# One chunk of attention moved to 64-row matmuls with three swaps of row tiles, and the u loads moved to another queue

## Chip, cores, metric

One core of a Trainium2 chip. The metric is the device time of one execution in microseconds (us). The profile's engines are PE (TensorE), DVE (VectorE), ACT (ScalarE), POOL (GpSimd) and SP (SyncE). A "q" behind an engine is its sequencer; the number behind L is a line of that run's kernel, so the same statement has other numbers before and after.

## The reference, cut to what matters

```python
# batch 8, seq S = 3008, d_model 256, d_qk 64; d_ff 2048
scores = (1.0 / S) * (z @ z.T)            # per batch
attn   = np.maximum(scores, 0.0) ** 2
x      = u * (attn @ v)                   # gated attention, (8*3008, 256)
h      = x @ w_in
out    = (h * sigmoid(1.702 * h)) @ w_out
```

The queries go in chunks of 512 (six a batch), the keys in 24 blocks of 128; the last key block holds 64 rows. A "score unit" is a pair of key blocks against one chunk. Scores are symmetric, so a chunk takes the blocks left of its diagonal from transposed squares of earlier chunks (tiles `tt`, made by DMA transposes that SyncE issues).

## The kernel before

`post` and `behind` are the only ordering between the two array halves: `post` is a GpSimd instruction that waits for the last matmuls of one half assignment, and `behind` makes the first matmuls of the next wait for it.

```python
TOP, LOW, FULL = slice(0, SREM), slice(SREM, P), slice(0, P)      # 0:64, 64:128, 0:128

def post(last):
    sig = pool.nop()
    for m in last:
        tc.add_manual_dep(sig.ins, m.ins.name, SYNC, reason="row tiles of one bank")
    return sig

def load_u(b, i):
    eng = pool if b or i else sp
    # ... four DMAs into uq (two buffers)

def scores(b, group):        # 64-row matmuls: two per unit, side by side in the array
    # ... pe.matmul(sc[:, r, :], zt[r * 64:(r + 1) * 64, key block], zt[same rows, chunk])

def square(b, i, jp, sc):    # ScalarE: relu(sc) -> rl; VectorE: rl * rl -> a; then, for some, a transpose of a into tt

def attend(b, i, both=False):
    # ... js: the key blocks in this chunk's order; cs: the two halves of the 256 channels
    half = [(0, TOP, NJ - 1), (1, LOW, NJ - 1)]
    if both:                 # chunks 0 and 1 of batch 0
        order = [[(c, FULL, j)] for j in js[:-CB] for c in cs] + [[(c, FULL, j)] for c in cs for j in js[-CB:]]
        order.insert(-CB, half)
    elif i == full(b):
        ...
    else:                    # all blocks in one half assignment, swap, all blocks in the other
        order = [[(0, TOP, j), (1, LOW, j)] for j in js] + [half] + [[(1, TOP, j), (0, LOW, j)] for j in js]
    acc, turn = {}, -1 if both or i == full(b) else NJ
    def step(k):
        for m in order[k]:
            # ... ins = pe.matmul(acc[c], V16[h, j] (channels c), weights(b, i, j)[h])
            if k == turn:
                behind(acc["sig"], ins)
        if k == turn - 1:
            acc["sig"] = post(done)

SCHED0 = {                   # chunk: {step: score units issued ahead of it}
    1: {0: 2, 8: 2, 15: 2, 22: 2, 30: 2, 38: 2},
    # ...
}
LOAD0 = {(1, 14): 2, (2, 12): 3, (2, NJ + 20): 4, (4, 8): 5}      # (chunk, step): u tile to load
LOADW = {(2, 16): 0, (2, 30): 1, (3, 9): 2, (3, 41): 3, ...}      # quarters of w_in, from GpSimd

# in the main loop, for every batch:
if i == 3 and n in (3, 26) and LAST2:
    LAST2.pop(0)()           # two late stores of the batch before, from SyncE's queue
```

## Time and profile before

| | before |
|---|---|
| time, median of 3 at first | 1180.64 us (1180.62 to 1186.32) |
| PE busy | 99% of the span |
| chunk 1, first score to the next chunk's first score | 37.64 - 23.36 = 14.28 us |
| transposes of `tt` in the first 80 us, issue to landing | 5.2 us median, 8.9 at most |

TensorE is the bound. The prediction shows its lines.

### The profile page before, as it was taken

How to read it: one execution, taken by the hardware profiler on the slowest of the kernel's cores; microseconds unless marked ns; L12 is line 12 of the kernel's file. 1: busy time of each engine (PE TensorE's matmuls, PEld its weight loads, DVE VectorE, ACT ScalarE, POOL GpSimd, SP SyncE). 2: the span in 40 equal slices, each digit the busy share in tenths (PEclk: the TensorE clock that was granted, in tenths of full speed). 3: DMA queues.
4: the chain of work that ended last, by engine and by line, in shares of the span. 5: the costliest groups of instructions: out<-in, count | busy, mean ns of one | idle time of the engine just before them, and what ended most of it. 6: DMA issues, size and time to landing. Idle time of an engine off the chain costs nothing.

```text
span 1178.7 us, 23495 instructions
## 1 busy us (share of the span) xinstructions
PE 1172.5 (99%) x9238; PEld 667.2 (57%) x9238; DVE 870.7 (74%) x1455; ACT 849.6 (72%) x1033; POOL 222.1 (19%) x313
## 2 busy tenths in 40 slices
PE   9999999999999999999999999999999999999998
PEld 3446664466644675446654467544674446744566
DVE  6779866878758786587875878658786587764776
ACT  7888874688746887478864787647876478772785
POOL 5243101231012310132101431014100241001000
PEclk9999999999999999999999999999999999999999
DMA  9998679877698677976879668896578965796023
GB/s 226 217 120 125 133 116 160 91 112 135 106 156 100 108 135 130 150 91 95 147 128 149 94 93 157 139 137 94 94 135 135 141 106 97 127 158 127 1 37 73
DMA packets 449696, 143.66 MB, mean 122 GB/s; under 512 B 414640, under 2 KB 443056, under 8 KB 449584
## 3 DMA queue, kind: packets, MB, share of 16 engines
q1 hardware_dynamic: 392160, 99.80, 51.2%
q0 software_dynamic: 56064, 41.04, 23.1%
q8 instruction: 72, 1.18, 0.4%
q10 hardware_dynamic: 1360, 1.31, 0.4%
q14 instruction: 40, 0.33, 0.1%
HBM read 60.29 MB, written 24.64 MB: 72 GB/s over the span
## 4 chain that ended last, share of the span: by engine, by line
PE 99%; ACT 1%; issue 0%; DVE 0%
PE o L358 40%; PE hg L399 27%; PE st L523 23%; PE sc L235 6%; PE st L526 1%; PE yp L497 1%; PE w L99 0%; ACT rl L256 0%; ACT W L443 0%; ACT gf L407 0%; PE zp L135 0%; ACT ZT L143 0%; ACT zst L126 0%; DVE y L544 0%; DVE nil L75 0%
## 5 line engine op out<-in xcount | busy, mean ns | idle before, releaser
L407 ACT ACTIVATE gf<-hg 128x1024 f32<-128x1024 f32 (+1 forms) x384 | 385.5, 1004 | 113.6 <-PE hg L399 98.3
L256 ACT ACTIVATE rl<-sc 128x1024 f16<-128x1024 f32 (+1 forms) x301 | 287.5, 993 | 145.4 <-PE sc L235 101.2
L358 PEld LDWEIGHTS <-V 64*128 64x128 f16 (+1 forms) x4052 | 217.7, 94 | 253.9 <-issue 11.8
L399 PE MATMUL hg<-xt,W 128*128 128x512 f16 (+1 forms) x1408 | 354.6, 374 | 0.2
L358 PE MATMUL o<-a,V 64*128 64x512 f16 (+3 forms) x2240 | 296.0, 368 | 0.0
L411 DVE TENSOR_SCALAR gt<-gf 128x1024 f16<-128x1024 f32 (+1 forms) x288 | 203.0, 705 | 114.0 <-ACT gf L407 112.8
L195 POOL DMA_DIRECT2D uq<-in_u_dram x188 | 125.2, 674 | 751.8 <-PE sc L235 527.5
L270 DVE TENSOR_TENSOR a<-rl 128x1024 f16<-128x1024 f16 (+1 forms) x266 | 177.6, 670 | 112.3 <-ACT rl L256 111.0
L358 PE MATMUL o<-tt,V 64*128 64x512 f16 (+1 forms) x1510 | 232.2, 377 | 0.0
L399 PEld LDWEIGHTS <-W 128*128 128x128 f16 x1536 | 149.4, 98 | 125.6 <-issue 2.6
L523 PEld LDWEIGHTS <-WT 128*128 128x128 f16 x1472 | 139.1, 98 | 45.1
L523 PEld LDWEIGHTS <-W 128*128 128x128 f16 x1104 | 104.7, 98 | 32.2
L235 PE MATMUL sc<-ZT 64*128 64x512 f16 (+3 forms) x688 | 115.5, 357 | 0.5 <-ACT ZT L143 0.3
L409 ACT ACTIVATE gt<-gf 128x1024 f16<-128x1024 f32 (+1 forms) x96 | 98.9, 1030 | 3.0
L540 ACT ACTIVATE y<-st 128x256 f32<-128x256 f32 x192 | 70.8, 369 | 35.7 <-PE st L523 29.2
L523 PE MATMUL st<-gt,WT 128*128 128x256 f16 (+1 forms) x736 | 91.9, 268 | 0.0
L523 PE MATMUL st<-s,WT 128*128 128x256 f16 (+1 forms) x736 | 90.8, 268 | 0.0
L523 PE MATMUL st<-gt,W 128*128 128x256 f16 (+1 forms) x736 | 90.8, 268 | 0.0
L544 DVE SCALAR_TENSOR_TENSOR y<-st,y 128x256 f32<-128x256 f32 (+1 forms) x144 | 57.7, 407 | 24.3 <-ACT y L540 11.7
L375 DVE TENSOR_TENSOR xt<-o,ut 128x512 f16<-128x512 f32 x80 | 51.3, 683 | 28.5 <-PE o L358 28.5
L477 DVE TENSOR_TENSOR s<-s,gt 128x1024 f16<-128x1024 f16 (+1 forms) x96 | 63.7, 663 | 1.1
L475 DVE TENSOR_TENSOR s<-gt 128x1024 f16<-128x1024 f16 (+1 forms) x96 | 63.3, 660 | 0.0
(59 smaller groups left out, 668.5 us busy)
## 6 DMA issues: line engine op xcount, KB each, us to landing
uq<-in_u_dram POOLq DMA_DIRECT2D x156, 128.0 KB, 3.6
out_dram<-yo SPq DMA_DIRECT2D x156, 128.0 KB, 2.8
V<-in_v_dram POOLq DMA_DIRECT2D x35, 256.0 KB, 6.4
tt<-a SPq DMA_TRANSPOSE x232, 3.4
uq<-in_u_dram POOLq DMA_DIRECT2D x32, 112.0 KB, 5.4
out_dram<-yo SPq DMA_DIRECT2D x28, 96.0 KB, 6.0
wst<-in_moe_w_in_dram POOLq DMA_DIRECT2D x4, 512.0 KB, 6.2
vst<-in_v_dram SPq DMA_DIRECT2D x3, 512.0 KB, 5.4
```

Of the source, the lines that this page charges most:

```text
L195: eng.dma_start(uq[k * QW:(k + 1) * QW, :n // QW].rearrange("t q c k -> t q (c k)"), src[:, :, cs])
L235: pe.matmul(sc[:, r, :q1 - q0], zt[h, 2 * kp + r, :], zt[h].rearrange("d n p -> d (n p)")[:, q0:q1], start=True, stop=True,)
L256: act.activation(rl[:, :, :n], sc[:, :, :n], AF.Relu, scale=csc)
L270: dve.tensor_tensor(a[:, :, :n], rl[:, :, :n], rl[:, :, :n], ALU.mult)
L358: ins = pe.matmul(acc[c][:, :n], V16[b][h, j].rearrange("p (c k) -> p k c", k=NCC)[:, c], weights(b, i, j)[h], start=(k, m) == first[c], s ...
L399: pe.matmul(hg[:, e, :n], W1[:, c, ff * P:(ff + 1) * P], XT[b, i][:, c, :n], start=(c == 0), stop=(c == NCC - 1),)
L407: act.activation(gf[:, :, :n], hg[:, :, :n], AF.Gelu_apprx_sigmoid, scale=1.0 / FSC)
L409: act.activation(g, gf[:, :, :n], AF.Copy, scale=FSC)
L411: dve.tensor_scalar(g, gf[:, :, :n], FSC, None, ALU.mult)
L477: dve.tensor_tensor(s_, ST[b, k, "S1", h], a11, ALU.subtract)
L523: pe.matmul(bank, right[:, ff], lhs()[:, f], start=first, stop=last, skip_group_check=True)
L540: act.activation(y[:, c, :, o], bank, AF.Copy, scale=1.0 / FSC)
```

## The change

A 64-row matmul uses half of the rows of TensorE's array, a "row tile", so that two of them run side by side; a "swap" exchanges which half of the array adds to which output bank.

Intent: of the three 128-row chunks of the first batch, chunk 1 goes to 64-row matmuls, so that TensorE need not change mode around each score group. Its score units come while the chunk runs, so not all key blocks are there in the first half of it; therefore the blocks go in groups, with three swaps at steps 8, 22 and 38, each behind two score units. The first batch's u tiles come from SyncE's queue, which frees GpSimd for the swap signals, and the second weight quarter is held until chunk 2 is done.

```diff
     def load_u(b, i):
-        eng = pool if b or i else sp
+        eng = pool if b else sp
@@ attend
-        if both:
+        turns = [NJ]
+        if (b, i) == (0, 1):
+            x, y = ([(0, TOP), (1, LOW)], [(1, TOP), (0, LOW)])
+            parts = [(x, js[:8]), (y, js[:14]), (x, js[8:]), (y, js[14:])]
+            order = [[(c, h, j) for c, h in cfg] for cfg, part in parts for j in part]
+            order.insert(37, half)
+            turns = [8, 22, 38]
+        elif both:
@@ step
-                if k == turn:
+                if k in turns:
                     behind(acc["sig"], ins)
-            if k == turn - 1:
+            if k + 1 in turns:
                 acc["sig"] = post(done)
@@ load_w
-        if k == 0:
-            hold = const.tile([P, 1], F16, name="hold")
-            pool.tensor_copy(hold, XT[0, 1][:, 0, :1])
+        if k < 2:
+            hold = const.tile([P, 1], F16, name=f"hold{k}")
+            pool.tensor_copy(hold, XT[0, k + 1][:, 0, :1])
@@ LOADW
-        (2, 16): 0, (2, 30): 1, (3, 9): 2, ...
+        (2, 16): 0, (3, 0): 1, (3, 9): 2, ...
@@ ahead of the main loop
-    load_u(0, 1)
@@ main loop
-            for n, step in enumerate(attend(b, i, b == 0 and i < 2)):
-                if b == 0 and i == 0 and n == 5:
-                    load_u(0, 0)
+            for n, step in enumerate(attend(b, i, b == 0 and i == 0)):
+                if b == 0 and i == 0 and n in (5, 24):
+                    load_u(0, n // 24)
```

More of the change, by code (lines that the diff above doesn't have):

```diff
@@ L349, in attend @@
         final = {c: [m for m in flat if m[1][0] == c][-1] for c in cs}
-        acc, turn = {}, -1 if both or i == full(b) else NJ
+        acc = {}
+        if both or i == full(b):
+            turns = []
         def step(k):
@@ L623 @@
     LOADW = {
-        (2, 16): 0, (2, 30): 1, (3, 9): 2, (3, 41): 3, (4, 28): 4, (4, 34): 5, (4, 40): 6, (5, 0): 7,
+        (2, 16): 0, (3, 0): 1, (3, 9): 2, (3, 41): 3, (4, 28): 4, (4, 34): 5, (4, 40): 6, (5, 0): 7,
     }
```

## The prediction

> **What bounds the kernel now.** I read the page's busy shares and the chain that ended last first, then the matmul engine's timeline over the first two chunks of the first batch, then ScalarE's and GpSimd's over the same stretch.
>
> ```profile
> PE 1172.5 (99%) x9238; PEld 667.2 (57%) x9238; DVE 870.7 (74%) x1455; ACT 849.6 (72%) x1033; POOL 222.1 (19%) x313
> ...
> PE 99%; ACT 1%; issue 0%; DVE 0%
> ```
>
> TensorE is 99% of the span and 99% of the chain, at a granted clock of 1.00. So only what shortens PE's own stream counts, and a microsecond taken out of it shows at the end unless a later wait eats it. The "busy" hides something, though: modelled matmul ends overlap the next start, so a pause of 0.1 us between two matmuls counts as busy. Start times show it. Here is chunk 1 of batch 0 (start, length, instruction group):
>
> ```profile
> 23.36 0.61 PE L235 MATMUL sc<-ZT 64*128 64x512 f16 x4
> 23.89 1.90 PE L358 MATMUL o<-tt,V 128*128 128x512 f16 x8
> 25.73 0.61 PE L235 MATMUL sc<-ZT 64*128 64x512 f16 x4
> 26.27 1.69 PE L358 MATMUL o<-a,V 128*128 128x512 f16 x7
> 27.88 0.66 PE L235 MATMUL sc<-ZT 64*128 64x512 f16 x4
> 28.47 1.69 PE L358 MATMUL o<-a,V 128*128 128x512 f16 x7
> 30.09 0.61 PE L235 MATMUL sc<-ZT 64*128 64x512 f16 x4
> 30.63 1.90 PE L358 MATMUL o<-a,V 128*128 128x512 f16 x8
> 32.46 0.61 PE L235 MATMUL sc<-ZT 64*128 64x512 f16 x4
> 33.00 1.90 PE L358 MATMUL o<-a,V 128*128 128x512 f16 x8
> 34.84 0.60 PE L235 MATMUL sc<-ZT 64*128 64x512 f16 x4
> 35.37 2.33 PE L358 MATMUL o<-a,V 128*128 128x512 f16 x10
> 37.64 0.39 PE L235 MATMUL sc<-ZT 64*128 64x512 f16 x2
> ```
>
> The next chunk already runs in 64-row mode:
>
> ```profile
> 41.10 2.75 PE L358 MATMUL o<-a,V 64*128 64x512 f16 x24
> 43.69 0.59 PE L235 MATMUL sc<-ZT 64*128 64x512 f16 x4
> 44.12 1.03 PE L358 MATMUL o<-a,V 64*128 64x512 f16 x8
> 44.99 0.38 PE L358 MATMUL o<-tt,V 64*128 64x512 f16 x2
> ```
>
> Two 64-row matmuls start together, so I count "passes" of 512 columns: one full matmul, or one pair of 64-row ones. The x24 group is 12 passes in 43.69-41.10 = 2.59 us, 0.2158 us a pass. A full matmul costs the same within a mode. But in chunk 1 the cycle from score group to score group is 25.73-23.36 = 2.37 us for 8 full passes and 2 score passes, which at 0.2158 would be 2.16: 0.21 us more. The x7 cycle 25.73 to 27.88 is 2.15 against 9 x 0.2158 = 1.94, again 0.21. The loss is per trip out of full mode and back, not per pass. In chunk 2 there is none: 44.12 to 44.99 is 4 passes in 0.87 us, and the score group before it took 0.43 for 2.
>
> **What the Trainium skill says.** "TensorEngine Tiling (Array Packing)", Key Properties: changing the tiling mode, not just the tile, drains TensorE. The trace agrees: 0.21 us per round trip. The same page, Gotcha 1: different row tiles cannot access one PSUM bank at once and software must synchronize; that is why the 64-row order keeps each half of the array on its own output bank and needs a signal when the halves are exchanged. "TensorE: Matmul & The Clock Gate", Part 3, The mechanism: tiles of different row groups overlap, starting about 4 ns apart; the trace agrees, with a pair taking one pass of 0.2158 us. "DMA: Bandwidth & Descriptors", Issuing engines are not separate DMA queues: moving an issue only saves the issuing sequencer's time, the 16 engines stay shared. For the u move I rely on that; here one u issue takes 0.65 us of GpSimd and 0.48 to 0.57 us of SyncE.
>
> **The change part by part.**
>
> *Chunk 1's attention in 64-row mode.* The work is unchanged: 46 block-passes plus the half block is 47, plus 12 score units of one pass each, 59 passes, 59 x 0.2158 = 12.73 us. The chunk takes 37.64-23.36 = 14.28 us. The excess is 1.55 us: six trips to the score groups and one to the half block inside the x10 group (its cycle, 34.84 to 37.64, is 2.80 against 11 x 0.2158 = 2.37, so 0.43, two trips), 7 x 0.21 = 1.49, and a wait of 0.05 in the group at 27.88 (0.66 where the others take 0.61). The change removes all seven; the one switch on leaving chunk 0 lies before 23.36 and stays, with some 0.01 us of it in the first score pass. TensorE gets 94 attention matmuls for 48, so the matmul count goes 9238 to 9284, at no cost in time.
>
> *Three swaps.* At steps 8, 22 and 38 (and score units also at 0, 15 and 30) the halves are exchanged. Each swap waits for the last pair, by way of a GpSimd signal. Chunk 2's swap, shown above, is the same thing under the same cover of two score units: last pass, 0.43 us of scores, next pass at 44.12 with no hole. I put the three swaps at 0, if GpSimd is free (below).
>
> *What the faster stream runs into: ScalarE.* It must empty two score banks per group:
>
> ```profile
> 26.16 1.94 ACT L256 ACTIVATE rl<-sc 128x1024 f16<-128x1024 f32 x2 [0.43 <-PE sc L235]
> 28.32 1.94 ACT L256 ACTIVATE rl<-sc 128x1024 f16<-128x1024 f32 x2 [0.22 <-PE sc L235]
> ```
>
> ScalarE starts 0.43 after a score group does and is done 1.94 later; about 0.05 after that the group's second bank can be written. So the second unit of the next group may start no sooner than 2.42 us after the first unit of this one (25.73+2.42 = 28.15, which is where the 0.05 wait comes from: it wanted to start at 28.11). After the change, groups 8 steps apart are 10 passes = 2.16 us, the second unit wants to start at 2.37: waits 0.04 to 0.05. Groups 7 steps apart, 8 to 15 and 15 to 22, are 9 passes = 1.94, second unit at 2.16 to 2.19: a wait of about 0.23 to 0.26 for the first. It pushes the group itself back, so the interval to 22 is already ScalarE's own pace (1.94) and costs about nothing more. From 22 to 30 0.05 again, then nothing. Sum: 0.035 + 0.23 + 0.045 = 0.31 us. ScalarE's total of 12 x 0.97 = 11.6 us for the chunk stays under 12.7, so it doesn't become the bound of the chunk, only of this spot.
>
> New length: 12.73 + 0.01 + 0.31 = 13.05 us. Gain 14.28 - 13.05 = 1.23 us.
>
> *GpSimd, the u and weight loads.*
>
> ```profile
> 17.21 2.71 POOL L195 DMA_DIRECT2D uq<-in_u_dram  x4
> 22.72 2.58 POOL L195 DMA_DIRECT2D uq<-in_u_dram  x4 [2.80 <-DVE ut L202]
> 34.63 2.58 POOL L195 DMA_DIRECT2D uq<-in_u_dram  x4 [9.33 <-DVE ut L202]
> ```
>
> GpSimd runs in order, so a signal stuck behind an issue that waits would stop TensorE. After the change: signal 1 at about 25.3, then the loads of u chunk 2 (their buffer was released at 22.7 already), 4 x 0.65 = 2.6 us to about 28.1; signal 2 is due at about 29.5, signal 3 at about 33. Both find GpSimd idle. Chunk 1's own u, from SyncE, is issued after the transposes that end at 19.2 and lands well before it is turned (33.1 before, some 0.8 us sooner now). The second weight quarter moves from 44.6 to the end of chunk 2, about 49.8; a quarter takes 5.5 to 7.3 us to land, so by 57, and its cast stands at 61.56 now, 60.3 then. None of this is on the path: 0.
>
> *Beyond.* Everything after 37.64 starts 1.23 us sooner. PE has no wait for a DMA anywhere later in this trace, and batches 1 to 7 are untouched. I keep the whole 1.23: 1180.64 - 1.23 = 1179.4.
>
> **Rivals.**
> 1. *The swap signal becomes the new wait.* For: each goes TensorE, GpSimd, TensorE, and GpSimd issues loads between signals 1 and 2. Against: 1.4 us of slack there, and chunk 2's swap shows no hole. If each of the three cost 0.4 us, the gain would be eaten: 1180.6.
> 2. *ScalarE or VectorE paces chunk 1 more than I think.* VectorE is busy 10.5 of the 14.28 us, including a transposition of 1.24 us, and a late square holds a ScalarE output buffer. That would cost another 0.2 to 0.5: 1179.7 to 1179.9.
> 3. *Transfers give it back.* The DMA engines are near full up to 70 us, that load doesn't shrink, and demands come 1.23 us sooner. Transposed tiles take 3.4 us from issue to landing over the kernel, up to 8.9 here. Those of chunk 1's first blocks, issued from 25.6 on, are needed by chunk 2 at about 38.8; those of chunk 2's, issued at 37 to 40, by chunk 3 near 52.6. There are some microseconds of slack at each, and the weight casts follow ScalarE's order, not their landing. If it did bite, 1179.8 to 1180.6. A better result (1179.1) would need ScalarE's wait to be absent.
>
> **Range and chances.** The mechanism is measured in this trace and its ceiling is the 1.55 us of excess (1179.1); only the ScalarE wait and the swaps are uncertain. The three times before are 1180.62, 1180.64 and 1186.32, so repeats usually agree to 0.02 but one can lie far off. 1178.9 to 1180.7 should hold the median 8 times in 10. A gain of 0.1% cannot reach 2% (23.6 us) either way: within 2% 0.99, slower 0.005, faster 0.005.
>
> **What would show it.** In the changed profile: in chunk 1 only 64x512 attention groups, score groups of 4 lasting 0.59 instead of 0.61, and the chunk from first score to next chunk's first score 13.05 us; a longer score group (about 0.8) at step 15; no hole after the score groups at steps 8, 22 and 38; PE x9284; u issues on GpSimd 184 instead of 188. I am wrong on the swaps if attention starts over 0.5 us after its score group there; wrong on ScalarE if step 15's group shows no wait or several groups do; wrong on the rest if chunk 1 shrinks by 1.2 us and the span doesn't, with a new wait for tt, W or ut in chunks 2 to 4.

## The result and the profile after

Six runs: 1180.38 us median (1179.89 to 1181.13), beside 1180.55 before (1180.33 to 1186.32 over six). The ratio of the fast runs is 0.9992, 95% interval 0.9975 to 1.0009: the same. (That of the medians quoted here would be 0.9999.) The time lies in the predicted range, but of the 1.23 us that the prediction wanted to keep, the medians show 0.17. Times alone settle nothing at this size: the interval is some 2 us wide to each side, and what follows is read from one profiled run of each kernel.

Chunk 1 did what was predicted. The timeline of TensorE after (start, length, group):

```profile
23.24 0.61 PE L235 MATMUL sc<-ZT 64*128 64x512 f16 x4
23.68 1.03 PE L367 MATMUL o<-tt,V 64*128 64x512 f16 x8
...
27.38 0.83 PE L235 MATMUL sc<-ZT 64*128 64x512 f16 x4
28.03 1.69 PE L367 MATMUL o<-a,V 64*128 64x512 f16 x14
29.54 0.66 PE L235 MATMUL sc<-ZT 64*128 64x512 f16 x4
30.02 1.90 PE L367 MATMUL o<-a,V 64*128 64x512 f16 x16
...
36.32 0.40 PE L235 MATMUL sc<-ZT 64*128 64x512 f16 x2
```

36.32 - 23.24 = 13.08 us, for 14.28 before: 1.20 us less. The group at 27.38 is step 15's, with ScalarE's wait in it (0.83 for 0.61). Behind the swap group at 29.54 attention goes on after 0.48 us, with no hole.

Matched matmul by matmul, the changed kernel is 1.32 us ahead at 36.32 (0.12 of it from before chunk 1, within what that start varies from run to run), and it is still 1.33 ahead at the last batch's chunk 4, where its score pair starts at 1075.26 and that of before at 1076.59. One score pair later it is ahead by only 0.21 (1081.31 and 1081.52). The timeline of before there:

```profile
1080.23 0.60 PE L358 MATMUL o<-ad,V 64*128 64x512 f16 x4
1080.66 1.03 PE L358 MATMUL o<-tt,V 64*128 64x512 f16 x8
```

and of after:

```profile
1078.90 0.59 PE L367 MATMUL o<-ad,V 64*128 64x512 f16 x4
1080.44 1.04 PE L367 MATMUL o<-tt,V 64*128 64x512 f16 x8 [0.94 <-DMA tt<-a]
```

Four 64-row matmuls are two passes, 0.43 us; 1078.90 + 0.43 = 1079.33, so TensorE stood for 1.11 us, waiting for a transposed tile. The chain of waits after shows the way to it (start, length, what):

```profile
1073.18 0.63 DVE a L270
...
1075.24 0.47 SPq L599
...
1075.83 4.57 DMA tt<-a
```

The square was ready at 1073.95 (after a small second VectorE step), four stores stood ahead in SyncE's queue until 1075.7, and the transpose took 4.57 us. In the kernel before it was issued 1.44 us later (1077.27) and took 3.14, so it landed at the same 1080.4. Why did it take longer? The DMA view of the stretch 1077 to 1079.5 us after has one 16 KB transfer of the instruction queue that the view of 1077.3 to 1080.4 before doesn't have. Its row of digits is the busy share of the DMA engines in 40 slices, the row below what they moved:

```profile
DMA  7799999999999999991990000001000100100000
GB/s 140 152 188 193 221 213 209 229 471 233 205 213 225 197 209 164 119 66 25 29 8 0 0 0 0 0 0 8 4 8 8 12 8 8 12 8 8 8 12 12
...
q8 instruction: 1, 0.02, 2.9%
```

The fetch begins at 1077.56 and takes 1.17 us; some twenty of the transpose's 256-byte packets, which take 20 ns elsewhere, end only after 1.3 to 1.6 us; then the engines move almost nothing until 1079.5. While before's transpose was under way, no 256-byte packet took over 0.1 us. The whole trace of after says the same: of the 385,408 such packets in the same hardware queue 488 took over 1 us, and 466 of these began during one of the 72 fetches, which cover 79 us of the 1178. (Not every fetch does it: 25 of the 72 held up ten packets or more.) That suggested theory A: the gain was real, and a fetch of TensorE's instructions, shifted by the change onto the last tight transpose, gave it back.

"Runtime: NRT & Kernel Launch", Instruction fetch mechanics, in the Trainium skill says that instructions are refilled in 16 KiB blocks of 256, each sequencer driving its own DMA queue. The trace agrees: 72 such transfers for TensorE's 2 x 9284 weight loads and matmuls, one per 258. The change adds 46 matmuls and 46 weight loads, 92 instructions, so each later fetch comes 92 instructions earlier in the program. In 64-row mode four instructions take 0.2158 us, so 92 take some 5.0; with the 1.3 us lead, the fetch at 1083.6 before should come near 1077.3. It came at 1077.6.

### The profile page after: what moved, and what is told of

Its sections match the earlier page's. It is cut to its first block, busy times and chain, and to the rows that moved or that the text cites. A ratio compares the mean times of both kernels' runs of the same rounds, so it can differ in the third digit from the quotient of the medians.

```text
span 1178.3 us, 23585 instructions
## 1 busy us (share of the span) xinstructions
PE 1171.0 (99%) x9284; PEld 670.0 (57%) x9284; DVE 871.0 (74%) x1455; ACT 849.4 (72%) x1033; POOL 209.4 (18%) x294
## 4 chain that ended last, share of the span: by engine, by line
PE 98%; ACT 1%; DMA 0%; issue 0%; SPq 0%; DVE 0%
PE o L367 40%; PE hg L408 28%; PE st L532 23%; PE sc L235 6%; PE st L535 1%; PE yp L506 1%; ACT rl L256 0%; DMA tt<-a 0%; PE w L99 0%; ACT W L452 0%; SPq L599 0%; ACT ZT L143 0%; ACT gf L416 0%; PE zp L135 0%; DVE a L270 0%
## 5 line engine op out<-in xcount | busy, mean ns | idle before, releaser
L420 DVE TENSOR_SCALAR gt<-gf 128x1024 f16<-128x1024 f32 (+1 forms) x288 | 200.1, 695 | 114.2 <-ACT gf L416 113.1
L195 POOL DMA_DIRECT2D uq<-in_u_dram x168 | 111.7, 673 | 739.9 <-PE sc L235 537.1
L553 DVE SCALAR_TENSOR_TENSOR y<-st,y 128x256 f32<-128x256 f32 (+1 forms) x144 | 57.7, 408 | 24.5 <-ACT y L549 11.5
```

Source lines behind the costliest of these rows:

```text
L195: eng.dma_start(uq[k * QW:(k + 1) * QW, :n // QW].rearrange("t q c k -> t q (c k)"), src[:, :, cs])
L420: dve.tensor_scalar(g, gf[:, :, :n], FSC, None, ALU.mult)
```

## The experiments

All outputs are right. The chips of these sessions were less quiet: the kernel before itself ranged from 1180.24 to 1194.73 (clock 0.993 to 1.000), so runs of one kernel spread by several us. In the profiles chunk 1 starts anywhere from 22.91 to 23.82 us. I therefore quote lowest and median times with those of before in the same rounds. At 2% no run differs from before; only rows_only (ratio 1.0051, 1.0021 to 1.0081) and best (1.0038, 1.0008 to 1.0068) have an interval that leaves out 1. The two kernels run once, in an unknown state, are used for their traces alone.

| run | times, us: lowest / median | before, same rounds | chunk 1, us | wait in the last batch, us |
|---|---|---|---|---|
| after | 1179.89 / 1180.38 | 1180.33 / 1180.55 | 13.08 | 1.11 |
| after_split82 | 1179.05 / 1180.90 | 1180.44 / 1181.87 | 13.09 | 0 |
| before_split46 | 1181.55 / 1182.31 | 1180.44 / 1181.87 | 14.29 | 1.02 |
| after_store | 1179.72 / 1180.25 | 1180.44 / 1181.87 | 13.18 | 0 |
| before_store | 1180.05 / 1181.39 | 1180.44 / 1181.87 | 14.28 | 0 |
| rows_only | 1182.37 / 1188.69 | 1180.27 / 1180.50 | 13.08 | 1.2 |
| loads_only | 1179.89 / 1181.49 | 1180.27 / 1180.50 | 14.29 | 0 |
| bare_swaps | 1180.04 (one run) | 1180.27 / 1180.50 | 13.96 | 0 |
| best | 1182.20 / 1186.62 | 1180.27 / 1180.50 | 12.87 | 0 |
| rows_early_u | 1180.40 / 1181.68 | 1180.24 / 1180.73 | 13.08 | 1.0 |
| no_hold | 1180.93 / 1181.53 | 1180.24 / 1180.73 | 13.09 | 1.5 |
| even_store | 1178.93 / 1179.59 | 1180.24 / 1180.73 | 12.87 | 0 |
| one_swap | 1180.95 (one run) | 1180.24 / 1180.73 | 14.99 | 0 |

Only the second matmul of each pair is split here.

### Is it the fetch? More instructions, and nothing else

```diff
     def up_group(b, q):
+            two = b == 1 and SPLIT[0] > 0      # SPLIT = [82] on after, [46] on before
+            SPLIT[0] -= two
             for c in range(NCC):
-                pe.matmul(hg[:, e, :n], ...)
+                for x0, x1 in [(0, CH // 2), (CH // 2, n)] if two and c else [(0, n)]:
+                    pe.matmul(hg[:, e, x0:x1], ...)
```

> The changed kernel with 82 of batch 1's up-projection matmuls cut into two of half the columns, so 164 more TensorE instructions (82 weight loads, 82 matmuls). With the change's own 92 that makes 256, and theory A says that TensorE's instructions come in blocks of 16 KB, about every 256 instructions, so every later fetch falls at the same point of the program as in the kernel before. Theory A (the gain of chunk 1 is lost again to a 1.1 us wait in the last batch, because an instruction fetch of 16 KB falls onto the last transposes there): the wait near 1080 us is under 0.2 us, no fetch between 1074 and 1081 us, time 1179.2 to 1179.5 (splits cost at most 0.3 us). Theory B (the wait comes from the stores that stand before the transpose in SyncE's queue, and a faster TensorE simply arrives earlier than the data): the wait stays near 1 us, time 1180.2 to 1180.6.

> The kernel before with 46 such cuts in batch 1: 92 more TensorE instructions, as many as the change adds, and nothing else of the change. Theory A: the fetch now falls onto the last transposes, at about 1079 us, and TensorE waits 0.5 to 2 us for the transposed tile in the last batch, where it waited 0; time 1181 to 1182.5. Theory B: no such wait, time 1180.5 to 1180.9.

TensorE's timeline of after_split82 and then of before_split46:

```profile
1078.92 0.60 PE L367 MATMUL o<-ad,V 64*128 64x512 f16 x4
1079.35 1.03 PE L367 MATMUL o<-tt,V 64*128 64x512 f16 x8
```

```profile
1080.80 0.60 PE L358 MATMUL o<-ad,V 64*128 64x512 f16 x4
1082.25 1.04 PE L358 MATMUL o<-tt,V 64*128 64x512 f16 x8 [0.85 <-DMA tt<-a]
```

The transpose in their DMA views, in the same order (the last number is us from issue to landing):

```profile
tt<-a SPq DMA_TRANSPOSE x1, 3.0
```

```profile
tt<-a SPq DMA_TRANSPOSE x1, 4.5
```

In after_split82 the fetches come at 1071.4 and 1082.2, the transpose is issued at 1075.86, at the same place behind the same stores as in the changed kernel, and lands in 3.05 us instead of 4.57; the wait is gone, and its three lowest runs are 1179.05, 1179.12 and 1179.67 (1179.2 to 1179.5 was expected). In before_split46 a fetch comes at 1079.8, the transpose lands in 4.5 us, and the kernel before, with nothing else of the change in it, has a wait of 1.02 us like the changed kernel; its lowest run is 1.1 us over that of before. Both directions go theory A's way and against theory B. So do all kept traces that have the stores where they were: the five with a fetch during this transpose (after, before_split46, rows_only, rows_early_u, no_hold) took 4.4 to 4.9 us to land it and waited, the three without one (before, after_split82, loads_only) took 3.05 to 3.4 us and did not. The three other runs of after_split82 (1182 to 1185) are within what before itself did in that session.

### The other remedy: move the stores that stand ahead of the transpose

```diff
-                if i == 3 and n in (3, 26) and LAST2:
+                if i == 3 and n in (3, 38 if b == B - 1 else 26) and LAST2:
```

> The changed kernel, with the second late store of the last batch's chunk 3 moved from step 26 to step 38, behind the last transpose of that chunk in SyncE's queue. Theories A and B: the transpose is issued at about 1074 instead of 1075.8 us and lands before TensorE needs it at 1079.4, whether or not a fetch comes at 1077.6; no wait; time 1179.1 to 1179.4. Theory C (something else holds the last tile up, such as the landing of earlier transfers): the wait stays, 1180.2 or more.

> The kernel before with the same store moved. It has no wait there, so theories A and B both say that nothing is gained: 1180.4 to 1180.6, and the last transpose lands 1.5 to 2 us earlier than before. If it gains over 0.3 us, the store cost something that I have not seen.

Neither profile has the wait: the last `tt` lands 1.66 us (after_store) and 1.79 us (before_store) ahead of its use, for 0.25 before. In after_store it landed at 1081.99, just ahead of a fetch at 1082.08 (everything ran 3 us late there), so the moved store kept the two apart; what it would do under a fetch was not tried. The lowest run is 1179.72, not the 1179.1 to 1179.4 expected: the mechanism came out, the size not quite. before_store gained 0.4 us in the lowest run, over the 0.3 that I had named, but inside that session's spread: open. The two profiled runs were long ones (1183.34 and 1184.89); that of after_store shows a weakness of the moved loads. From 50 to 85 us (who waited for whom, total, times, longest):

```profile
DVE ut L202 <- DMA uq<-in_u_dram: 3.9, 1, 3.9
...
ACT rl L256 <- DVE a L270: 2.6, 1, 2.6
PE hg L408 <- ACT rl L256: 2.5, 1, 2.5
```

A u tile in SyncE's queue stands behind transposes; when these are slow, it lands late (61.99 here), VectorE waits to turn it, ScalarE waits for VectorE and TensorE for ScalarE.

### What the moved loads are for

rows_only takes the attention part of the diff alone. loads_only takes the rest alone.

> Chunk 1's 64-row order and its three swaps as in the change, with every load of u and of the weights as before (u from GpSimd, second weight quarter held by nothing). If the 64-row order alone makes the gain: chunk 1 from its first score to the next chunk's first score takes 13.0 to 13.1 us, as in the changed kernel. If the loads had to move so that GpSimd can pass the swap signals on (my rival 1): a hole behind the score groups at step 8 or 22, chunk 1 13.5 us or more. TensorE has the changed kernel's instruction count, so an instruction fetch should again fall onto the last transposes of the last batch: a wait of 0.5 to 1.5 us near 1080 us, time 1180.0 to 1180.8 on a quiet chip.

> The kernel before with the moved loads alone (all of the first batch's u from SyncE's queue, the hold on the second weight quarter). Chunk 1 stays at 14.2 to 14.4 us; the fourth u tile lands at 53 to 58 us instead of 41 because it stands behind SyncE's transposes; no wait in the last batch, since TensorE's instruction count is that of the kernel before. Time as before within 0.3 us if the loads cost nothing; 1 to 3 us more in those runs where the late u tile holds VectorE up.

rows_only makes chunk 1 as short as the change does (23.11 to 36.19 us), with no hole behind a swap: the signals pass through GpSimd in time. My rival 1 is refuted. Yet all six of its runs are longer than before's median, by 8 us in their own median and 2.1 in the lowest. The time goes at 62 to 82 us. Waits of rows_only there (who waited for whom, total, times, longest):

```profile
DVE a L270 <- DMA tt<-a: 5.1, 2, 3.7
...
PE o L367 <- DMA tt<-a: 3.8, 2, 3.3
```

The view of tile `tt` over the first 80 us ends with its transposes' time to landing; rows_only first, then after:

```profile
DMA to landing us min/median/max: 3.1/8.8/15.6
```

```profile
DMA to landing us min/median/max: 3.2/4.6/7.0
```

GpSimd's timeline of rows_only shows where it starts:

```profile
26.24 2.58 POOL L195 DMA_DIRECT2D uq<-in_u_dram  x4 [6.55 <-DVE a L270]
```

In the program the first swap signal stands ahead of this load of the third u tile, so GpSimd, which could have issued it at 22.7, as before, waits for chunk 1's step 7 (the releaser that the profile names is a guess; the trace has the signal at 25.48 us, with this load right behind it) and issues it on top of SyncE's transposes, which start at 25.3. loads_only did as expected: chunk 1 14.29 us, the fourth u tile landing at 54.1 to 57.7, and no gain. To see whether the position of that one load is enough, I moved it ahead of the signal:

```diff
-    LOAD0 = {(1, 14): 2, ...           # on rows_only
+    LOAD0 = {(1, 6): 2, ...
```

> rows_only with one number changed: GpSimd's load of the third u tile stands ahead of the first swap signal (step 6 of chunk 1 instead of 14), so that it can be issued at 22.5 us as in the kernel before, not at 26.2 behind the signal. Theory D1 (rows_only lost 8 us because the signal pushed this load onto SyncE's transposes, which then fell behind for good): the transposes of the first 80 us take about 5 us to land as before (median) instead of 8.8, no waits of TensorE for tt at 62 to 82 us in the profiled run, most runs 1180 to 1181 with the last batch's fetch wait of about 1 us. Theory D2 (the faster TensorE itself asks for transposes that GpSimd's loads always delay): as slow as rows_only, median over 1184.

Issued at 22.44 us, landing of `tt` 6.1 us median for 8.8, no wait of TensorE for `tt` between 60 and 84 us, median 1181.68 for 1188.69 (another chip, the same lowest before within 0.03 us). Theory D1 holds for the most part: one load on the wrong side of a signal made most of that 7 us. Not all came as expected: only two of the six runs lie at 1180 to 1181, and the landing stays over the 5 us expected and the changed kernel's 4.6. (The run of 1198.79 was slow, at a granted clock of 0.992, and says nothing here; without it the median is 1181.60.) That GpSimd's loads beside transposes stay a risk is a guess. The runs of the noisy sessions point that way, without being an experiment on it: of 33 runs of the kernel before 14 are over 1182 us, the worst 1194.73; of the 32 runs of kernels with u from SyncE 9 are, the worst 1184.85.

The hold on the second weight quarter, removed from the changed kernel:

> The changed kernel with the second weight quarter loaded as before (at step 30 of chunk 2, no second hold), u from SyncE. If the hold is what keeps the transposes on time: median landing of the first 80 us over 6 us and time over 1182. If u's move to SyncE's queue does it alone, as I expect: landing 4.4 to 5 us, 1180.2 to 1180.8, like the changed kernel.

Landing 4.9 us, as expected for u's move doing the work. The median is 0.7 us above the top of what I gave; the profiled run has 1.5 us of wait in the last batch, more than after's 1.11. No run of after stands in that session, so whether the hold is worth anything stays open.

### What a swap costs, and why there are three

bare_swaps moves the swaps off the score groups, to 10, 26 and 40, with groups of blocks to match; one_swap has a single swap at step 24 and score groups at 0, 5, 10, 15, 24, 32. Both have the moved store.

> The changed kernel with the three swaps moved off the score groups, to steps 10, 26 and 40 (groups of 10, 16, 13 and the half block, 7), and the late store of the last batch behind its transposes. Each swap now waits uncovered for TensorE, GpSimd, TensorE: from chunk 2's swap, where the weight load behind the signal starts 0.49 us after the last pair, I estimate a hole of 0.38 us each. Chunk 1: 12.74 + 3 x 0.38 + 0.04 = 13.9 us. If the signal is much cheaper than that (under 0.1 us each), 13.1 us.

> The changed kernel with one swap at step 24 as in the later chunks, which needs every key block in the first half; so the score groups come at steps 0, 5, 10, 15, then 24 and 32. ScalarE's 1.94 us per group against 7 passes = 1.5 us: waits of about 0.2, 0.4 and 0.4 us at the groups at 5, 10 and 15, and 0.5 us or so before step 20 for a square just made. Chunk 1 about 14.2 us, so all of the gain lost again. If it is under 13.3, three swaps were not needed.

bare_swaps, its first swap (step 10):

```profile
26.01 0.61 PE L367 MATMUL o<-a,V 64*128 64x512 f16 x4
26.73 1.04 PE L367 MATMUL o<-tt,V 64*128 64x512 f16 x8
```

Two passes would end at 26.44; the next start at 26.73 leaves 0.29 us, as at the other two swaps, less than my 0.38. ScalarE's wait stayed, at step 22, so the chunk came to 13.96, near the 13.9 from partly wrong terms. The cover of two score units (0.43 us) is worth three times 0.29. one_swap needed 14.99 us, worse than the 14.2 I gave and than the old order: waits of 0.68, 0.33 and 0.35 us between a group's two score pairs, on ScalarE, then 0.35 and 0.48 on VectorE's squares. Of the groupings tried, only those with three covered swaps make the 64-row mode pay in full; two swaps were not tried.

### Versions to beat both

```diff
-            parts = [(x, js[:8]), (y, js[:14]), (x, js[8:]), (y, js[14:])]     # and half at 37
-            turns = [8, 22, 38]
-        1: {0: 2, 8: 2, 15: 2, 22: 2, 30: 2, 38: 2},
+            parts = [(x, js[:8]), (y, js[:16]), (x, js[8:]), (y, js[16:])]     # and half at 39
+            turns = [8, 24, 40]
+        1: {0: 2, 8: 2, 16: 2, 24: 2, 32: 2, 40: 2},
```

Both have the moved store; best has GpSimd's loads (rows_only), even_store those of the change.

> rows_only with two more edits: the score groups and swaps evenly spaced (scores at 0, 8, 16, 24, 32, 40; swaps at 8, 24, 40), which takes away ScalarE's wait of 0.2 us, and the last batch's late store behind its transposes. Chunk 1 12.8 to 12.95 us, no score group over 0.66 us; no wait near 1080 us; on a quiet chip 1179.0 to 1179.3, so 1.2 to 1.5 us under the kernel before of the same rounds.

> The changed kernel, loads and all, with the evenly spaced score groups and swaps (0, 8, 16, 24, 32, 40 and 8, 24, 40) and the last batch's late store behind its transposes. Chunk 1 12.87 us as in the run called best, no wait in the last batch: its undisturbed runs at 1179.0 to 1179.3, against 1180.3 to 1180.6 of the kernel before; it should be the fastest of all.

Chunk 1 takes 12.87 us in both, and no score group is over 0.66 us: ScalarE's long wait was a matter of spacing (its short ones of about 0.04 stay). best was sent off before I had rows_only's result and has its sickness: my 1179.0 to 1179.3 was wrong by 7 us in the median. even_store has the lowest times of all, 1178.93 lowest and 1179.59 median beside 1180.24 and 1180.73; one of its six runs (1179.14) lies in the range that I gave. The last `tt` lands at 1078.39 there, 1.58 us ahead of its use and just ahead of a fetch at 1078.44, because the stores now follow it:

```profile
1072.56 3.30 SPq L298 DMA_TRANSPOSE tt<-a  x2
1075.95 2.28 SPq L599 DMA_DIRECT2D out_dram<-yo  x4
```

Its profiled run (1179.67) still waits 0.7 us for a `tt` at 74 us, in the first batch's crowded stretch. Its ratio is 0.9973 (0.9935 to 1.0011), so over that session's noise the gain of 0.1% is not established by the times; the removed waits are seen in its profiled run.

## Why the prediction was right or wrong

- *Seven mode changes at 0.21 us are the excess.* Right: with them gone, only the terms below are left, and the chunk fell by 1.20 us of a predicted 1.23. (7 x 0.21 is 1.47, not 1.49; the new length does not rest on it.)
- *ScalarE's wait of 0.31 us.* Right in place and size: step 15's group took 0.83 us for 0.61, the others 0.61 to 0.66; start by start the waits are 0.22 there and 0.13 in three other groups, 0.35 in all, and the chunk 13.08 for a predicted 13.05. Even spacing took 0.21 of it away.
- *Three covered swaps cost nothing.* Right. Uncovered, they cost 0.29 us each (I had 0.4 as a fear and 0.38 as an estimate).
- *GpSimd, and the u loads: "None of this is on the path: 0".* I misread the diff: all of the first batch's u moves to SyncE, not chunk 1's alone, so GpSimd has 168 u issues after, not the 184 that I forecast. And while the moved loads gain nothing by themselves (loads_only), the 64-row order without them is 8 us slower than before in the median, about 1 us with one load put earlier (rows_early_u). The loads behind signal 1 that I put at 0 are, but for details, those of rows_only (issued from 26.24 us): for the kernel that I thought I was judging the 0 was wrong by 8 us, and that the real change has no such loads is luck. My rival 1 looked for the damage at the signal; it sits with the load that the signal delays. Rival 3 named the right kind of tile but gave them some microseconds of slack.
- *"Batches 1 to 7 are untouched. I keep the whole 1.23."* This step failed. Their text is untouched, but 92 more TensorE instructions moved each later instruction fetch, and one fell onto the last batch's last tight transpose, which took 4.57 us for 3.14: 1.11 us of the 1.32 us lead lost. Before, that tile had landed only 0.25 us ahead of its use (1080.41, used at 1080.66). "PE has no wait for a DMA" was true of the trace and told nothing of the slack; I should have asked which tile lands last before its use.
- The range held, the point was 1.0 us too low; in the traces nearly all of it is this one term. That the range held is luck as far as the mechanism goes: it reached up to no gain at all (1180.64) for other reasons, and the fetch was in none of the rivals.

## What to carry to other kernels

When the bound engine gets faster, look through the rest of the trace for transfers that land just ahead of their use: with 0.25 us of slack, a landing that took 1.4 us longer cost a wait of 1.11. Changing an engine's instruction count moves all its later instruction fetches, so a far-away gain or loss of about 1 us can be that alone; pad or cut to the same count before one explains it. A signal put into a queue that also issues loads delays the loads behind it, and the damage shows tens of microseconds later.

## What the Trainium skill lacked or had wrong

- "Runtime: NRT & Kernel Launch", Instruction fetch mechanics: it calls the cost of a block boundary one DMA tail-bump, mostly hidden. Hidden for the fetching engine here (the chain has 0% of "issue"), but a 16 KB fetch (1.17 us) beside a DMA transpose held some of its packets for 1.3 to 1.6 us instead of 20 ns, and made its landing 4.57 us instead of 3.05 without the fetch; not on the page.
- "TensorEngine Tiling (Array Packing)", Key Properties: it says that a mode change drains TensorE, not what that costs. Here 0.21 us for a trip from 128-row matmuls to 64-row ones and back; and 0.29 us for an uncovered exchange of row tiles by way of another engine's signal, on which the page gives no time.
- "DMA: Bandwidth & Descriptors", Rules for kernel authors: a transpose next to ordinary DMAs "needs nothing". The row is about the data being right; the page gives no time for a transpose beside other transfers. With the third u tile's load from GpSimd at 26.24 us, on top of them, the first 80 us' transposes took 8.8 us (median) to land, with the same load at 22.44 us 6.1, in the kernel before (22.72 us) 5.2, and with these loads in the transposes' own queue 4.6 (4.9 without the second hold).
- No page that I read says how to place instruction fetches in time; here 92 more TensorE instructions and a lead of 1.3 us brought one from 1083.6 to 1077.6 us.
